# Two-stage attention and a gated short convolution on one core: output products as four 32-channel column strips, last stores joined, another order

## The chip, the cores and the metric

The kernel runs on one core of one Trainium2 chip. The metric is the device time of one execution in microseconds, lower is better. The program has one launch; host code only brings the inputs into another layout.

## The reference, cut to what matters

`B, N, C = 4, 12800, 128`, 32 inducing points, all in f32:

```python
def mab(q, kv):
    s = scale * (q @ kv.transpose(0, 2, 1)); s = s - s.max(-1, keepdims=True)
    a = np.exp(s); a /= a.sum(-1, keepdims=True) + 1e-09
    return a @ kv
h = mab(I, x)            # 32 inducing points attend to all tokens: (4, 32, 128)
y = mab(x, h)            # each token attends to the 32 rows of h: (4, 12800, 128)
gate_pre = sum(conv_w[k] * y_shifted_by(4 - k) for k in range(5))
out = (sigmoid(gate_pre) * (y @ w_val)) @ w_out
```

## The kernel before, in words

Each batch's 12800 tokens are four strips of 3200 (`R = 4`), which lie side by side on the partitions, 32 partitions to a strip. The 3200 are cut into 7 or 8 chunks (`SIZES`, 128 to 512 tokens of each strip); there are 29 chunks `k` over the four batches.

Per batch: `s1` makes the first scores of a chunk (f32, four matmuls of 32 columns, one to each token strip), DVE copies them out with their maximum; `gm` takes the maximum over a group of chunks (`GROUPS`) on POOL; `e1`/`h` take the exponential on ACT, transpose 32 x 32 blocks on DVE and multiply with x (again 32-column strips). `x` turns x on PE for batch 0, later batches load it in both layouts. `u`, `t`, `w`, `W` (`prep` to `prep3`) make h, its transpose hT, and the weights W that carry h, the convolution and the value projection; `po` (`prep_out`) scales the output weights and splits them into f16 high and low parts. `s2` makes the second scores of a chunk (f32 strips) and sends them down a chain: DVE transpose and maximum (L697, L702), POOL subtract (L708), ACT exponential (L714), DVE sum (L720), POOL multiply (L731), DVE transpose (L737), ACT and POOL split into f16 high and low parts P1 and P2 (L742, L749).

A row block `r` (`rblock`, two per chunk) multiplies W with shifted P in matmuls of 32 rows by 128 columns, four at a time on the four row groups: 15 terms of the gate (L763) and 3 of the value (L772). ACT takes the tanh (L833), DVE multiplies gate and value (`gv`, L843), ACT and POOL split that into f16 parts gh and gl (L856, L861).

`o` (`outp`) is the output product of one token strip of a chunk: three f16 terms, 128 rows by 128 columns (L881 to L883), for the last chunk one f32 product (L874). ACT or DVE (`OUTV` says which) copies it out of PSUM with its scale (L893, L891), and SP stores it (L898). So PE has three tile shapes, which the planner calls full (128 x 128), rows (32 x 128) and strips (128 x 32).

The order is a planner's. PE runs the items of the table `ORDER` as they stand; `z` is a run of dummy products on zeros (first number: its name, second: how many). All other engines get their order from a list schedule with assumed durations, due times and the biases `URGE`; `AHEAD` bounds how early loads go. Each engine runs its queue strictly in that order and waits on semaphores.

Of the kernel before, what the change touches and what calls it, by code (L numbers as in the profile page):

```python
# [20 lines left out]
P = 128  # L21
# [28 lines left out]
class Plan:  # L50
# [85 lines left out]
    def lay(self, deps, succ, topo, nominal):  # L136
# [18 lines left out]
        while len(seq) < n:  # L155
# [14 lines left out]
            if e == "SP":  # L170
                bus = max(bus, start) + ops[i]["dur"]
                end[i] = max(bus, start + 0.5) + (1.7 if start < 10.0 else 2.6)
                free[e] = start + 0.4
# [39 lines left out]
def tile_kernel(ctx: ExitStack, tc: tile.TileContext, xt, xk, indT_in, w64, out):  # L213
# [288 lines left out]
    def prep(b):  # L502
# [27 lines left out]
        i2 = PE(0.21 * len(gs) + 0.05, f3, [i0] + [ix["sum", b, c] for c in range(len(SIZES[b]))], [key], Hs + Ds, lag=0.2)  # L530
# [28 lines left out]
    def prep2(b):  # L559
# [4 lines left out]
        def f4():  # L564
            T.matmul(pt(key)[:, :M], c_["wval"], st["hT", b], start=True, stop=True)

        i4 = PE(0.28, f4, [ix["hT", b], iw], [key], [("hT", b)], lag=0.15)
# [46 lines left out]
    def prep3(b, e):  # L614
# [8 lines left out]
        i6 = PE(0.35, f6, ix[w2][e], [key], [w2], lag=0.25)  # L623
# [240 lines left out]

    def outp(k, r):
        b, c = seqs[k]
        n, p, q = SIZES[b][c], r // 2, r % 2
        g1, g2, tg = ("gh", b, c, p), ("gl", b, c, p), ("tg", b, c, p)
        key, os = ("a", "o", b, c, r), ("os", b, c, r)
        if k >= len(seqs) - 2:  # L870
            os = ("ss" if k == len(seqs) - 1 else ("et", "et", "et", "pt")[r], "out", b, c, r)
        if k == len(seqs) - 1:
            def f():
                T.matmul(pt(key)[:, :n], st["wof", b], st[tg][:, q, :n], start=True, stop=True)  # L874

            i = PE(1.06 / 512 * n, f, [ix["gv", b, c, r], ix["wo", b]], [key], [tg, ("wof", b)])
        else:
            def f():
                t = pt(key)[:, :n]
                w = st["wo", b]  # L880
                T.matmul(t, w[:, 0], st[g1][:, q, :n], start=True, stop=False)  # L881
                T.matmul(t, w[:, 1], st[g1][:, q, :n], start=False, stop=False)  # L882
                T.matmul(t, w[:, 0], st[g2][:, q, :n], start=False, stop=True)  # L883

            i = PE(COST["out"] * n, f, [ix[g2], ix["wo", b]], [key], [g1, g2, ("wo", b)])
        v = 4 * k + r in OUTV

        def ev():
            o, a = sb(pw, os, [P, 512])[:, :n], st[key][:, :n]
            if v:  # L890
                V.tensor_scalar(o, a, st["osc", b], None, ALU.mult)  # L891
            else:
                S.activation(o, a, AF.Copy, scale=st["osc", b])  # L893

        j = op("DVE" if v else "ACT", cost("psum", n) + 0.07 if v else cost("act", n) + 0.06, ev, [i], 0.0, [os], [key, ("osc", b)])

        def store():
            nc.sync.dma_start(out[b, :, r, FIRST[b][c]:FIRST[b][c] + n], st[os][:, :n])  # L898

        op("SP", n * 512 / BW, store, [j], 0.0, [], [os])  # L900


# [7 lines left out]
    def idle(k, n):  # L910
# [3 lines left out]
        def f():  # L914
            t = pt(key, (P, 2, 512))[:, 0]
            for _ in range(n):
                T.matmul(t, c_["zero"][:, :P], c_["zero"], start=True, stop=True)  # L917

        PE(0.216 * n, f, [], [key])
# [36 lines left out]
GROUPS = [[[0, 1], [2, 3, 4], [5, 6, 7]], [[0, 1, 2, 3], [4, 5, 6]], [[0, 1, 2], [3, 4, 5, 6]], [[0, 1, 2], [3, 4, 5, 6]]]  # L956
ORDER = [
# [40 lines left out]
]  # L998
XEV = ["SSSV", "SVSS", "SVSS", "SSSV", "SSSS", "SSVS", "SVSS", "SSVS"]
URGE = {  # L1000
    "e1.f": -13,
    "s2.sub": 8,
# [81 lines left out]
```

## Time and profile before

| | us |
|---|---|
| three runs | 287.75, 288.19, 290.25 |
| median | 288.19 |
| the profiled execution | 288.69 |
| its span (first to last instruction) | 286.6 |
| PE, DVE, POOL, ACT busy | 278.0, 230.4, 214.2, 204.6 |

In the lines of the profile, PE is TensorE's matmuls, PEld its weight loads, DVE VectorE, ACT ScalarE, POOL GpSimd, SP the engine that issues most DMAs. A row in order of time has start and length in us, engine, line, operation, what it writes and reads, tile rows*columns, shape and count; in brackets stands the idle time ahead of it and what ended it. A matmul's length is longer than its share of PE's time, since matmuls overlap: the distance between starts is what counts. A row in 20 us stretches has the busy time of PE, PEld, DVE, ACT and POOL, then the granted clock, the DMA share and GB/s.

### The profile page before, as it was taken

What the parts mean: (1) busy time and instruction counts of PE and PEld (TensorE: products, weight loads), DVE (VectorE), ACT (ScalarE), POOL (GpSimd) and SP (SyncE); (2) the same over time, 40 slices, a digit from 0 to 9 for tenths busy, and PEclk for the clock granted to TensorE, in tenths of its full rate; (3) what the DMA queues carried; (4) which work ended last, traced back from release to release, by engine and by line L of the source; (5) the groups of instructions that cost most, each with busy time, mean ns of one, the idle gap of its engine ahead of it and who ended that gap; (6) DMA issues with size and microseconds to landing.
All of it is one profiled execution on the core that took longest, in us unless ns stands there. A gap on an engine that the chain in (4) does not pass through costs nothing.

```text
span 286.6 us, 10022 instructions
## 1 busy us (share of the span) xinstructions
PE 278.0 (97%) x4038; PEld 136.0 (47%) x4038; DVE 230.4 (80%) x574; ACT 204.6 (71%) x310; POOL 214.2 (75%) x256
## 2 busy tenths in 40 slices
PE   8899999999999999999999999999999999999992
PEld 3467546464335335555454645644334443433450
DVE  1458899999999999769789899897896986844551
ACT  2363344578785769767787579897799787888792
POOL 1122077887899989959498989998899999865770
PEclk9999999999999999999999999999999999999998
DMA  7999999999987979998647993234233343443545
GB/s 250 408 418 421 415 387 365 414 392 395 361 314 234 403 274 294 413 363 267 239 160 234 342 387 109 106 125 159 88 132 130 129 148 128 156 146 148 189 159 194
DMA packets 24382, 74.50 MB, mean 260 GB/s; under 512 B 2832, under 2 KB 12560, under 8 KB 22160
## 3 DMA queue, kind: packets, MB, share of 16 engines
q1 hardware_dynamic: 24192, 73.84, 69.0%
q8 instruction: 32, 0.52, 0.7%
q14 instruction: 14, 0.11, 0.1%
q10 hardware_dynamic: 144, 0.02, 0.0%
HBM read 47.63 MB, written 26.21 MB: 258 GB/s over the span
## 4 chain that ended last, share of the span: by engine, by line
PE 90%; DVE 4%; DMA 3%; issue 0%; SPq 0%; ACT 0%
PE g L763 29%; PE a L881 10%; PE a L486 8%; PE a L691 8%; PE a L883 7%; PE a L882 7%; PE a L772 7%; PE a L422 7%; PE g L397 3%; DMA xt<-in_xt_dram 3%; PE g L917 2%; PE a L621 1%; DVE ss L430 1%; DVE e L697 1%; PE a L528 1%; PE a L874 0%
## 5 line engine op out<-in xcount | busy, mean ns | idle before, releaser
L861 POOL TENSOR_TENSOR gl<-tg,gh 128x1024 f16<-128x1024 f32 (+4 forms) x56 | 106.5, 1906 | 18.0 <-ACT gh L856 15.7
L763 PE MATMUL g<-P,W 32*128 32x448 f16 (+5 forms) x1740 | 109.7, 345 | 0.0
L833 ACT ACTIVATE tg<-g,gsc 128x1024 f32<-128x1024 f32 (+5 forms) x58 | 57.8, 996 | 29.4 <-PE g L763 24.9
L843 DVE SCALAR_TENSOR_TENSOR tg<-tg,a 128x512 f32<-128x512 f32 (+5 forms) x116 | 65.5, 602 | 11.7 <-PE a L772 10.8
L763 PEld LDWEIGHTS <-W 32*128 32x128 f16 x1740 | 50.6, 92 | 43.2 <-issue 13.1
L856 ACT CAST gh<-tg 128x1024 f16<-128x1024 f32 (+4 forms) x56 | 52.7, 946 | 0.6 <-PE a L882 0.2
L772 PE MATMUL a<-P,W 32*128 32x512 f16 (+5 forms) x348 | 42.7, 348 | 0.0
L893 ACT ACTIVATE os<-a,osc 128x512 f32<-128x512 f32 (+4 forms) x63 | 38.1, 633 | 5.5 <-PE a L883 5.3
L881 PE MATMUL a<-gh,wo 128*128 128x512 f16 (+4 forms) x112 | 40.2, 359 | 0.0
L882 PE MATMUL a<-gh,wo 128*128 128x512 f16 (+4 forms) x112 | 39.6, 354 | 0.0
L883 PE MATMUL a<-gl,wo 128*128 128x512 f16 (+4 forms) x112 | 39.6, 354 | 0.0
L891 DVE TENSOR_SCALAR os<-a,osc 128x448 f32<-128x448 f32 (+4 forms) x45 | 29.6, 674 | 7.8 <-PE a L883 7.4
L749 POOL TENSOR_TENSOR P<-pt,P 128x512 f16<-128x512 f32 (+4 forms) x29 | 29.9, 1038 | 2.6 <-ACT P L742 2.4
L731 POOL TENSOR_TENSOR e<-e,z 128x512 f32<-128x512 f32 (+4 forms) x29 | 27.1, 938 | 4.9 <-DVE z L723 2.5
L708 POOL TENSOR_TENSOR e<-e,m 128x512 f32<-128x512 f32 (+4 forms) x29 | 27.1, 938 | 3.1 <-DVE m L702 3.0
L422 PE MATMUL a<-xt,indT 128*32 128x512 f32 (+5 forms) x232 | 27.3, 540 | 1.3 <-DVE ss L430 0.9
L486 PE MATMUL a<-xk,et 128*32 128x129 f32 x800 | 28.1, 275 | 0.4 <-issue 0.3
L486 PEld LDWEIGHTS a<-xk,et 128*32 128x32 f32 x800 | 23.3, 109 | 8.2 <-issue 3.7
L691 PE MATMUL a<-xt,hT 128*32 128x512 f32 (+4 forms) x232 | 27.0, 544 | 0.0
L430 DVE TENSOR_SCALAR_CACHE_REDUCE ss<-a 128x512 f32<-128x512 f32 (+5 forms) x29 | 17.4, 603 | 11.9 <-PE a L422 11.6
L714 ACT ACTIVATE e<-e 128x512 f32<-128x512 f32 (+4 forms) x29 | 16.5, 576 | 10.5 <-POOL e L708 10.4
L881 PEld LDWEIGHTS <-wo 128*128 128x128 f16 x112 | 10.9, 97 | 27.4 <-issue 18.2
(107 smaller groups left out, 326.0 us busy)
## 6 DMA issues: line engine op xcount, KB each, us to landing
xt<-in_xt_dram SPq DMA_DIRECT2D x11, 1024.0 KB, 7.8
out_dram<-os SPq DMA_DIRECT2D x36, 256.0 KB, 3.8
xk<-in_xk_dram SPq DMA_DIRECT2D x10, 903.0 KB, 7.9
out_dram<-os SPq DMA_DIRECT2D x40, 224.0 KB, 2.4
xt<-in_xt_dram SPq DMA_DIRECT2D x8, 896.0 KB, 9.4
xk<-in_xk_dram SPq DMA_DIRECT2D x6, 1032.0 KB, 8.5
xt<-in_xt_dram SPq DMA_DIRECT2D x6, 960.0 KB, 8.0
xk<-in_xk_dram SPq DMA_DIRECT2D x5, 967.5 KB, 9.7
```

Source lines behind the costliest of these rows:

```text
L422: T.matmul(s[32 * r:32 * r + 32, :n], c_["indT"], x[:, o:o + n // 32, r, :], start=True, stop=True)
L486: T.matmul(t[32 * s:32 * s + 32, :P + 1], e[:, 32 * i:32 * i + 32], x[:, m + i, :], start=i < R, stop=i >= nb - R)
L691: T.matmul(s[32 * r:32 * r + 32, :n], st["hT", b], x[:, m:m + nb, r, :], start=True, stop=True)
L763: T.matmul(st[f"g{r // 2}", b, c][:, r % 2, :n], st["W", b][q, w, k, :], st[("P1", "P2")[e]][q, o:o + n], start=u == 0, stop=u == len(taps ...
L772: T.matmul(st["a", "v", b, c, r][:, :n], st["W", b][q, w, TAPS, :], st[("P1", "P2")[e]][q, o:o + n], start=u == 0, stop=u == 2)
L833: S.activation(t[:, :, :n], st[f"g{p}", b, c][:, :, :n], AF.Tanh, scale=st["gsc", b])
L843: V.scalar_tensor_tensor(t, t, 1.0, st["a", "v", b, c, r][:, :n], ALU.add, ALU.mult)
L856: S.copy(sb(pw, g1, [P, 2, 512], F16)[:, :, :n], st[tg][:, :, :n])
L861: G.tensor_tensor(sb(pw, g2, [P, 2, 512], F16)[:, :, :n], st[tg][:, :, :n], st[g1][:, :, :n], ALU.subtract)
L881: T.matmul(t, w[:, 0], st[g1][:, q, :n], start=True, stop=False)
L882: T.matmul(t, w[:, 1], st[g1][:, q, :n], start=False, stop=False)
L883: T.matmul(t, w[:, 0], st[g2][:, q, :n], start=False, stop=True)
```

## The change

An output product is cut by channels into four column strips of 32, so that it has the shape of the scores; so are the small products of `prep2` (`wval` by hT), and the dummy products have 32 columns. The output of the last chunk goes into one tile per pair of strips and out by two stores in place of four; of the last chunk but one, the stores of strips that ACT copies are issued by ACT. `ORDER` and its companions (`GROUPS`, `XEV`, `URGE`, `OUTV`, `AHEAD`) are another set, and the planner's tables say "strips" for the products that changed.

```diff
+    def columns(t, terms):
+        for j, (w, x) in enumerate(terms):
+            for r in range(R):
+                T.matmul(t[32 * r:32 * r + 32], w[:, 32 * r:32 * r + 32], x, start=j == 0, stop=j == len(terms) - 1)
...
-                T.matmul(t, w[:, 0], st[g1][:, q, :n], start=True, stop=False)
-                T.matmul(t, w[:, 1], st[g1][:, q, :n], start=False, stop=False)
-                T.matmul(t, w[:, 0], st[g2][:, q, :n], start=False, stop=True)
+                columns(t, [(w[:, 0], st[g1][:, q, :n]), (w[:, 1], st[g1][:, q, :n]), (w[:, 0], st[g2][:, q, :n])])
...
+        if last:
+            if q:
+                def store():
+                    nc.sync.dma_start(out[b, :, r - 1:r + 1, FIRST[b][c]:FIRST[b][c] + n],
+                                      st[os][:, :2 * n].rearrange("p (r t) -> p r t", r=2))
...
+        elif k == len(seqs) - 2 and not v:
+            def store():
+                S.dma_start(out[b, :, r, FIRST[b][c]:FIRST[b][c] + n], st[os][:, :n])
...
-                T.matmul(t, c_["zero"][:, :P], c_["zero"], start=True, stop=True)
+                T.matmul(t[:M], c_["zero"][:, :M], c_["zero"], start=True, stop=True)
...
-GROUPS = [[[0, 1], [2, 3, 4], [5, 6, 7]], [[0, 1, 2, 3], [4, 5, 6]], [[0, 1, 2], [3, 4, 5, 6]], [[0, 1, 2], [3, 4, 5, 6]]]
+GROUPS = [[[0, 1, 2], [3, 4], [5, 6, 7]], [[0, 1, 2, 3], [4, 5, 6]], [[0, 1, 2], [3, 4, 5, 6]], [[0, 1, 2], [3, 4, 5, 6]]]
...
-    ("W", 2, 0), ("o", 11, 0), ("r", 13, 0), ("h", 3, 0), ("h", 3, 1), ("s1", 3, 6), ("s2", 2, 6), ("s2", 2, 4),
+    ("s2", 2, 2), ("r", 12, 0), ("o", 10, 2), ("o", 10, 3), ("o", 11, 0), ("o", 11, 1), ("h", 3, 0), ("s1", 3, 5),
+    ("s2", 2, 5), ("h", 3, 1), ("s2", 2, 4), ("l", 1, 2), ("s1", 3, 4), ("r", 12, 1), ("s1", 3, 6), ("s2", 2, 6),
...
-AHEAD = 19
+AHEAD = 25
```

Three places show what the change does to the queues. The first is PE in the middle of the program. Before, the last term of an output of batch 1 is followed by the second scores of batch 2 and a row block:

```order
L882 MATMUL a<-gh,wo 128x448
L883 LDWEIGHTS wo
L883 MATMUL a<-gl,wo 128x448
L691 MATMUL a<-xt,hT 32x480 x4
L763 LDWEIGHTS W
L763 MATMUL g_3042<-P_94,W 128x448
```

After, at the row block r(12,1) (the first number of a shape is the columns of the tile):

```order
L869 MATMUL a<-gl,wo 32x448
L486 MATMUL a<-xk,et 32x129 x15
L422 MATMUL a<-xt,indT 32x512 x4
L691 MATMUL a<-xt,hT 32x480 x4
L486 MATMUL a<-xk,et 32x129 x16
L691 MATMUL a<-xt,hT 32x448 x4
L422 MATMUL a<-xt,indT 32x512 x4
L772 LDWEIGHTS W
L772 MATMUL a<-P_94,W 128x448
```

Before, full, strips and rows follow each other; after, output, h, s1 and s2 are one run of strips up to the rows, and h, s1 and s2 stand here that stood behind r(13,0).

The second is DVE in the head, between hT of batch 0 and the first row block. Before (`e_603` and `e_623` are the second scores of chunks 0 and 1 of batch 0, `ss` the first scores of batch 1):

```order
L723 RECIPROCAL z_670<-z_670 128x8
L702 TENSOR_REDUCE m2_674<-e_667 128x16
L737 STREAM_TRANSPOSE pt_702<-e_603 128x160
L470 STREAM_TRANSPOSE et_710<-ss_529 128x448
L629 COPY W_713<-a_677 128x768
L697 STREAM_TRANSPOSE e_721<-a_704 128x512
L737 STREAM_TRANSPOSE pt_724<-e_623 128x256
```

After (`e_589` is chunk 1, `e_609` chunk 0):

```order
L702 TENSOR_REDUCE m2_715<-e_706 128x16
L470 STREAM_TRANSPOSE et_724<-ss_467 128x448
L470 STREAM_TRANSPOSE et_728<-ss_546 128x448
L470 STREAM_TRANSPOSE et_736<-ss_510 128x448
L737 STREAM_TRANSPOSE pt_739<-e_589 128x256
L737 STREAM_TRANSPOSE pt_756<-e_609 128x160
```

Three transposes of batch 1 moved ahead of the two that end the chain of chunks 1 and 0, and chunk 1 goes ahead of chunk 0.

The third is the tail, SP's last stores before:

```order
L898 DMA out_0_dram<-et_5761 128x512
L898 DMA out_0_dram<-ss_5767 128x160
L898 DMA out_0_dram<-ss_5772 128x160
L898 DMA out_0_dram<-ss_5774 128x160
L898 DMA out_0_dram<-ss_5781 128x160
L898 DMA out_0_dram<-et_5789 128x512
L898 DMA out_0_dram<-pt_5796 128x512
L898 DMA out_0_dram<-et_5799 128x512
```

and after, SP's:

```order
L924 DMA out_0_dram<-et_6762 128x512
L912 DMA out_0_dram<-ss_6777 128x2x160
L924 DMA out_0_dram<-et_6808 128x512
L912 DMA out_0_dram<-ss_6745 128x2x160
```

with two stores that went from SP to ACT's queue, where one copy stands ahead of the last of them:

```order
L905 ACTIVATE ss_6777<-a_6772,osc_4707 128x160
L918 DMA out_0_dram<-et_6769 128x512
L905 ACTIVATE pt_6815<-a_6794,osc_4707 128x512
L905 ACTIVATE ss_6745<-a_6810,osc_4707 128x160
L918 DMA out_0_dram<-pt_6815 128x512
```

More of the change, by code (lines that the diff above doesn't have):

```diff
@@ L172, in lay @@
                 end[i] = max(bus, start + 0.5) + (1.7 if start < 10.0 else 2.6)
-                free[e] = start + 0.4
+                free[e] = start + 0.45
             seq.append(i)
@@ L528, in f3 @@
                 T.matmul(t[:M, :P + 1], st[Ds[g]], st[Hs[g]], start=g == 0, stop=g == gs[-1])
-        i2 = PE(0.21 * len(gs) + 0.05, f3, [i0] + [ix["sum", b, c] for c in range(len(SIZES[b]))], [key], Hs + Ds, lag=0.2)
+        i2 = PE(0.21 * len(gs) + 0.05, f3, [i0] + [ix["sum", b, c] for c in range(len(SIZES[b]))], [key], Hs + Ds, "strips", lag=0.2)
         def f4():
@@ L564, in f4 @@
         def f4():
-            T.matmul(pt(key)[:, :M], c_["wval"], st["hT", b], start=True, stop=True)
-        i4 = PE(0.28, f4, [ix["hT", b], iw], [key], [("hT", b)], lag=0.15)
+            columns(pt(key)[:, :M], [(c_["wval"], st["hT", b])])
+        i4 = PE(0.28, f4, [ix["hT", b], iw], [key], [("hT", b)], "strips", lag=0.15)
         def g0():
@@ L621, in f6 @@
                     T.transpose(t[32 * r:32 * r + 32, q, :], st[w2][:, e, q, :], c_["ident"])
-        i6 = PE(0.35, f6, ix[w2][e], [key], [w2], lag=0.25)
+        i6 = PE(0.35, f6, ix[w2][e], [key], [w2], "strips", lag=0.25)
         def f7():
@@ L869, in outp @@
         key, os = ("a", "o", b, c, r), ("os", b, c, r)
-        if k >= len(seqs) - 2:
-            os = ("ss" if k == len(seqs) - 1 else ("et", "et", "et", "pt")[r], "out", b, c, r)
-        if k == len(seqs) - 1:
+        last = k == len(seqs) - 1
+        if last:
+            os = ("ss", "out", b, c, p)
+        elif k == len(seqs) - 2:
+            os = (("et", "et", "et", "pt")[r], "out", b, c, r)
+        if last:
             def f():
-                T.matmul(pt(key)[:, :n], st["wof", b], st[tg][:, q, :n], start=True, stop=True)
-            i = PE(1.06 / 512 * n, f, [ix["gv", b, c, r], ix["wo", b]], [key], [tg, ("wof", b)])
+                columns(pt(key)[:, :n], [(st["wof", b], st[tg][:, q, :n])])
+            i = PE(1.06 / 512 * n, f, [ix["gv", b, c, r], ix["wo", b]], [key], [tg, ("wof", b)], "strips")
         else:
@@ L880, in f @@
                 w = st["wo", b]
[L881 to L885, printed above, removed]
+                columns(t, [(w[:, 0], st[g1][:, q, :n]), (w[:, 1], st[g1][:, q, :n]), (w[:, 0], st[g2][:, q, :n])])
+            i = PE(COST["out"] * n, f, [ix[g2], ix["wo", b]], [key], [g1, g2, ("wo", b)], "strips")
         v = 4 * k + r in OUTV
+        new = not last or q == 0
         def ev():
-            o, a = sb(pw, os, [P, 512])[:, :n], st[key][:, :n]
+            if new:
+                sb(pw, os, [P, 512])
+            at = q * n if last else 0
+            o, a = st[os][:, at:at + n], st[key][:, :n]
             if v:
@@ L893, in ev, with store @@
                 S.activation(o, a, AF.Copy, scale=st["osc", b])
[L895 to L900, printed above, removed]
+        j = ix["out", k, r] = op("DVE" if v else "ACT", cost("psum", n) + 0.07 if v else cost("act", n) + 0.06, ev, [i], 0.0,
+                                 [os] * new, [key, ("osc", b)] + [os] * (not new))
+        if last:
+            if q:
+                def store():
+                    nc.sync.dma_start(out[b, :, r - 1:r + 1, FIRST[b][c]:FIRST[b][c] + n],
+                                      st[os][:, :2 * n].rearrange("p (r t) -> p r t", r=2))
+                op("SP", 2 * n * 512 / BW, store, [ix["out", k, r - 1], j], 0.0, [], [os])
+        elif k == len(seqs) - 2 and not v:
+            def store():
+                S.dma_start(out[b, :, r, FIRST[b][c]:FIRST[b][c] + n], st[os][:, :n])
+            j = op("ACT", 0.45, store, [j], 0.0, [], [os], lag=2.3)
+            op("NOP", 0.0, lambda: None, [j])
+        else:
+            def store():
+                nc.sync.dma_start(out[b, :, r, FIRST[b][c]:FIRST[b][c] + n], st[os][:, :n])
+            op("SP", n * 512 / BW, store, [j], 0.0, [], [os])
     def warm_up():
@@ L916, in f @@
             for _ in range(n):
-                T.matmul(t, c_["zero"][:, :P], c_["zero"], start=True, stop=True)
-        PE(0.216 * n, f, [], [key])
+                T.matmul(t[:M], c_["zero"][:, :M], c_["zero"], start=True, stop=True)
+        PE(0.216 * n, f, [], [key], kind="strips")
     def S1(b, c, bank="a"):
@@ L953, in tile_kernel @@
     return plan
-GROUPS = [[[0, 1], [2, 3, 4], [5, 6, 7]], [[0, 1, 2, 3], [4, 5, 6]], [[0, 1, 2], [3, 4, 5, 6]], [[0, 1, 2], [3, 4, 5, 6]]]
+GROUPS = [[[0, 1, 2], [3, 4], [5, 6, 7]], [[0, 1, 2, 3], [4, 5, 6]], [[0, 1, 2], [3, 4, 5, 6]], [[0, 1, 2], [3, 4, 5, 6]]]
 ORDER = [
[40 rows of a table removed]
[40 rows of a table added]
 ]
-XEV = ["SSSV", "SVSS", "SVSS", "SSSV", "SSSS", "SSVS", "SVSS", "SSVS"]
+XEV = ["SVVV", "SSSV", "SVSV", "SSSS", "SSSS", "SSVS", "SSSS", "SSSS"]
 URGE = {
-    "e1.f": -13,
-    "s2.sub": 8,
-    "s2.hi": -28,
-    "s2.lo": 7.5,
-    "s2.tout": -6.5,
-    "s2.ex": 1.5,
-    "s2.tin": -3.5,
-    "rblock.gv": -5,
-    "s2.sm": -2.5,
-    "make_xk.ev": 1.5,
-    "h.acc": -4,
-    "halves.lo": -1,
-    "s2.mx": 5.5,
-    "s1.g": -5.5,
-    "s2.nm": -3,
-    "halves.hi": -2,
-    "e1.tr": -4.5,
-    "evac.ev": -20.5,
-    "rblock.th": 8,
-    "values.gv": -4,
-    "rows.th": -8,
-    "gmax.f1": 4,
-    "gmax.f0": 1,
-    "outp.ev": 4,
+    "e1.f": -3,
+    "s2.sub": 14,
+    "s2.hi": -37.5,
+    "s2.lo": -0.5,
+    "s2.tout": -6,
+    "s2.ex": 3,
+    "s2.tin": 0.5,
+    "rblock.gv": -5,
+    "s2.sm": -2,
+    "make_xk.ev": 14,
+    "h.acc": -2,
+    "halves.lo": -0.5,
+    "s2.mx": 4.5,
+    "s1.g": -6.5,
+    "s2.nm": 9.5,
+    "halves.hi": -3,
+    "e1.tr": -2.5,
+    "evac.ev": -18.5,
+    "rblock.th": 9,
+    "values.gv": 5,
+    "rows.th": -6.5,
+    "gmax.f1": 28,
+    "gmax.f0": 1.5,
+    "outp.ev": 18,
 }
 TURNED = (0,)
-EVEN = 0.04765998428116873
+EVEN = 0.0469045735303122
 OUTV = [
[4 rows of a table removed]
[5 rows of a table added]
 ]
```

86 rows, old and new, of tables (ORDER, OUTV) are left out of this document.

## The prediction

> **What bounds the kernel now.** I read the page first (busy time, slices, the chain that ended last), then the stretches of 20 us, then the order of time on each engine.
>
> ```profile
> span 286.6 us, 10022 instructions
> PE 278.0 (97%) x4038; PEld 136.0 (47%) x4038; DVE 230.4 (80%) x574; ACT 204.6 (71%) x310; POOL 214.2 (75%) x256
> PEclk9999999999999999999999999999999999999998
> PE 90%; DVE 4%; DMA 3%; issue 0%; SPq 0%; ACT 0%
> ```
>
> The matrix engine is busy for 97% of the span, at the full granted clock, and the chain that ended last lies on it for 90%. So an edit is worth what it takes off PE, as long as no other engine comes to set PE's pace. Which one could is in the stretches (columns: PE, PEld, DVE, ACT, POOL):
>
> ```profile
> 40.00:60.00 20.00, 19.56 (x418) 11.20 (x415) 19.07 (x56) 10.64 (x22) 15.33 (x29) 1.00 0.98 390
> 60.00:80.00 20.00, 20.00 (x299) 9.49 (x302) 19.13 (x51) 15.39 (x27) 16.50 (x20) 1.00 1.01 377
> 80.00:100.00 20.00, 20.00 (x274) 8.42 (x270) 19.36 (x47) 14.32 (x20) 19.04 (x17) 1.00 0.86 312
> 120.00:140.00 20.00, 20.00 (x347) 10.39 (x335) 15.94 (x44) 14.40 (x23) 14.13 (x18) 1.00 0.92 323
> ```
>
> PE has no idle time from 60 us on, but in 40 to 100 us DVE is idle for only 2.4 us of 60: there it is nearly a second bound. In 120 to 140 us it has 4.1 us to spare.
>
> **Term 1: the changes of tile shape.** PE works in three shapes: full (outputs, transposes of x), rows (gate and value products, L763 and L772) and strips (scores, h, the turned weights). Between two shapes it stops:
>
> ```profile
> 149.91 0.35 PE L883 MATMUL a<-gl,wo 128*128 128x448 f16 x1
> 150.19 1.01 PE L691 MATMUL a<-xt,hT 128*32 128x480 f32 x8
> 151.72 1.30 PE L763 MATMUL g<-P,W 32*128 32x448 f16 x24
> 152.96 0.36 PE L881 MATMUL a<-gh,wo 128*128 128x448 f16 x1
> 154.29 0.35 PE L882 MATMUL a<-gh,wo 128*128 128x448 f16 x1
> 154.48 0.35 PE L883 MATMUL a<-gl,wo 128*128 128x448 f16 x1
> 154.76 0.36 PE L772 MATMUL a<-P,W 32*128 32x448 f16 x2
> 156.65 0.52 PE L621 MATMUL a<-ident,w 128*32 128x128 f16 x24
> 157.10 0.36 PE L881 MATMUL a<-gh,wo 128*128 128x448 f16 x1
> ```
>
> Within a shape a 448-wide product follows its predecessor after 0.19 us (154.29 to 154.48). From full to strips it takes 0.28 (149.91 to 150.19), so the change costs 0.09; from full to rows 0.28 (154.48 to 154.76), again 0.09; from rows to full, the 24 row products are six rounds of four, 6 x 0.19 = 1.14, and 1.24 pass to the output product: 0.10. From strips to full 0.45 pass, of which six rounds of 0.058 (worked out below) are work: 0.10.
>
> Now the price of an output product in strips: three terms by four strips, 12 matmuls in place of 3. It is unchanged only if four strips run at once, with their weight loads hidden. The trace has that form with the same data type, 128 rows by 32 columns in f16, in the turned weights:
>
> ```profile
> 41.90 0.52 PE L621 MATMUL a<-ident,w 128*32 128x128 f16 x24
> 42.25 1.89 PE L691 MATMUL a<-xt,hT 128*32 128x512 f32 x16
> 43.97 0.51 PE L621 MATMUL a<-ident,w 128*32 128x128 f16 x24
> L621 PEld LDWEIGHTS <-w 128*32 128x32 f16 x192 | 3.3, 96 | 3.1 <-issue 2.4 <-POOL e L708 0.3
> 56.60 0.22 PE L882 MATMUL a<-gh,wo 128*128 128x128 f16 x1
> 56.66 0.22 PE L883 MATMUL a<-gl,wo 128*128 128x128 f16 x1
> ```
>
> 24 strips of 128 columns take 0.35 us (41.90 to 42.25), six rounds of 0.058; one full product of 128 columns takes 0.06 (56.60 to 56.66). So four strips cost one full product, though each had its own weight load of 96 ns. The f32 strips that follow start with no gap: the data type alone costs nothing, which is what lets outputs join s1, s2 and h. I take the 336 rounds of the outputs at their old price. Bounds: 0, and for loads that don't hide, 336 x 0.096 = 32 us (a rival below).
>
> [...]
>
> Read from end to end in the two programs' orders, PE changes shape 169 times before (28 full to strips, 25 strips to full, 18 strips to rows, 15 rows to strips, 40 full to rows, 43 rows to full) and 131 times after (7, 6, 59, 59, 0, 0). I take 0.10 for each, as the two that remain (rows and strips) have it: 38 fewer are 3.8 us, 0.7 of it ahead of the first row block (19 changes against 12) and **3.1 us behind it**, where PE hardly waits, so these count in full. Bounds: at 0.09 out of full, 0.10 out of rows and 0.11 out of strips (the rows have two decimals) it is 16.7 against 13.7, 3.0 in all; at 0.11 throughout 4.2.
>
> **Term 2: the head.** The new order has 21 dummy products (`z`) for 31. Each is 0.22 us (18 of them fill 37.91 to 41.90 below), so 2.2 us of PE work go. Whether the time goes is decided by the first row block r(-1,1), which needs the probabilities P of chunk 0 and both halves of W:
>
> ```profile
> 35.47 0.28 POOL L456 TENSOR_SCALAR m<-m 64x1 f32<-64x1 f32 x1 [7.50 <-DVE m L441]
> 35.63 0.19 DVE L548 COPY hT<-a 128x32 f32<-128x32 f32 x1 [0.34 <-PE a L545]
> 36.20 1.00 POOL L450 TENSOR_SCALAR ng<-m 32x1 f32<-32x1 f32 x4
> 37.23 1.23 ACT L465 ACTIVATE ss<-ss,ng 128x448 f32<-128x448 f32 x2 [5.77 <-POOL ng L450]
> 37.91 4.06 PE L917 MATMUL g<-zero 128*128 128x512 f16 x18
> 42.21 0.60 DVE L470 STREAM_TRANSPOSE et<-ss 128x448 f32<-128x448 f32 x1
> 43.21 0.49 POOL L749 TENSOR_TENSOR P<-pt,P 128x160 f16<-128x160 f32 x1
> 44.00 0.40 DVE L737 STREAM_TRANSPOSE pt<-e 128x256 f32<-128x256 f32 x1
> 44.43 0.41 ACT L742 CAST P<-pt 128x256 f16<-128x256 f32 x1 [0.52 <-DVE pt L737]
> 44.92 0.67 POOL L749 TENSOR_TENSOR P<-pt,P 128x256 f16<-128x256 f32 x1 [1.22 <-ACT P L742]
> 46.14 1.02 PE L763 MATMUL g<-P,W 32*128 32x128 f16 x42
> ```
>
> Before, hT is there at 35.82 and P of chunk 0 at 43.70, 7.9 us later; r(-1,1) starts at 46.14. After, u comes earlier: four dummies (0.9) and one s1 chunk (0.75 by the 0.43 of a 512-wide f32 round, two rounds, scaled) less stand ahead of it, and the weights' load now lies ahead of the last x load; I take 1.4 us, hT at 34.4. But chunk 0's chain is longer: s2(0,1) goes first; POOL has the maximum of batch 1 (gm, 0.73 + 1.00) in the middle; ACT has four exponentials (0.62 each) ahead of P's casts; and DVE has three transposes L470 in a row ahead of L737. Counted from hT: the maximum enters POOL at about 4.1, ends at 5.8, the third exponential at 7.6; the three L470 fill 7.0 to 8.8; two L737 (0.4 and somewhat less) to 9.5; the casts to 9.9; the two L749 (0.67, 0.49) to **10.8**. So r(-1,1) starts at about 45.3: **0.85 us** gained of the 3.0 that the head could give (2.2 + 0.7 + 0.1 of other work moved). PE waits there for about 2 us, with only the rest of its queue behind it. Bounds: -3.0 (the chain is no longer than before) and +0.8 (it is 1.6 longer than counted). I take 0.85, since the queue orders are known and the durations are rows.
>
> **Term 3: the tail.**
>
> ```profile
> 280.93 0.38 PE L883 MATMUL a<-gl,wo 128*128 128x512 f16 x1
> 281.35 0.69 ACT L893 ACTIVATE et<-a,osc 128x512 f32<-128x512 f32 x1 [0.61 <-PE a L883]
> 279.23 2.81 SPq L898 DMA_DIRECT2D out_dram<-ss  x4
> 283.08 0.41 SPq L898 DMA_DIRECT2D out_dram<-et  x1
> out_dram<-et SPq DMA_DIRECT2D x3, 256.0 KB, 2.4
> out_dram<-ss SPq DMA_DIRECT2D x4, 80.0 KB, 3.2
> ```
>
> Before, PE's last product streams out at 281.15 (280.93 + 0.22). ACT's copy ends 0.9 later, but the last store is issued only at 283.08, behind a queue on SP that four small stores (2.81 us) had made; it lands after about 2.4, 4.4 us behind PE. After, two joined stores replace four, and two stores go out from ACT. The last work is o(28,1): its copy waits on ACT behind a 512-wide one (0.69), and ends about 1.0 behind PE; SP is free and issues at once. The joined store is of the small kind (3.2): 4.2 behind PE. **0.3 us** gained; between -1.0 (landing like the big ones, 2.4) and +0.5 (twice the rows of a small one, somewhat slower landing). An ACT-issued store holds ACT for about the 0.4 of these issues, with one copy queued behind it.
>
> **Term 4: other engines.** Their work is the same in sum (three more copies on DVE, one transposed block fewer). In 40 to 100 us DVE is the cover: PE gets some 1.3 us faster there by 13 or so fewer changes, and DVE has 2.4 us of idle time. I charge nothing; if the cover fails it is rival C.
>
> **The sum**: 3.1 + 0.85 + 0.3 = 4.25 off the profiled execution, whose own time is 288.69 (span 286.6 and 2.1 around it): 284.4. The median of the runs shown is 288.19, 0.5 below it, so in that frame **283.9**.
>
> **The rivals** (times in the median's frame).
> - B, the head keeps its whole gain: P of chunk 0 comes after 8 us as before. Another 2.2 us: 281.7. For it: before, z(2,18) ran on past the point at which the turned weights were ready. Against: the three L470 that now stand ahead.
> - C, DVE sets the pace between 46 and 100 us: the 1.3 us of that stretch and the head's 0.85 are lost: 286.1. For it: 19.1 to 19.4 of 20 busy. Against: DVE's queue has no more work ahead of each row block there than before.
> - D, the other side: ahead of r(12,1) stand now two s1, two s2 and two h that stood behind r(13,0). By their DVE work (transposes and reductions of about 0.6 to 0.7, nine or ten of them) gv of chunk 12 moves back by some 6 us. If DVE's idle time ahead (4.1 in 120 to 140) can't take any of it, since its inputs come too late, outputs of chunk 12 stall and PE with them: 283.9 + 6 = 290. It decides once less than 2 us of the 6 find idle time. Against: two row blocks lie between gv and those outputs.
> - E, the strips' loads stand open: 283.9 + 32 = 316. That is also the case in which the change doesn't do what it says. The rounds of L621 speak against it; they are 128 wide, and only more time is there at 512.
>
> **How the numbers follow.** My forecast 0.54 (own range 283.0 to 285.6), B 0.14, C 0.21, D 0.08, E 0.03. About 1%, 2.9 us, is what a measurement here can tell from no change: faster than 285.3 are most of the forecast and B (0.64), slower than 291.1 are a part of D, and E (0.06); the rest is within (0.30). The range from 281.5 to 287.6 takes in the forecast, most of B, and C, with the bounds of the tail.
>
> **What would show it.** Output products as 32-column strips whose rounds of four start 0.19 (448) or 0.22 us (512) apart; no gap where they meet s1, s2, h; gaps of about 0.1 only at row blocks, 59 each way; r(-1,1) near 45.3 us, with PE idle ahead of it; last store landing some 4.2 us behind PE. Rounds longer than 0.22 us mean E; idle PE ahead of row blocks in 46 to 100 us means C, around chunk 12 D. An idle PE in the last 80 us would be a thing that I have not foreseen.

## The result, and the profile after

The changed kernel takes 286.82 us in the median of 20 runs (284.49 to 288.74), the kernel before 288.97 beside it: ratio **0.9914, 95% interval 0.989 to 0.9938**, 2.5 us faster. The prediction had 4.3 us. The profiled execution took 286.78. From its page (the total, busy times, the chain, two groups, the queue of instruction packets, of which before had `32, 0.52, 0.7%`):

```profile
span 285.0 us, 12107 instructions
PE 274.5 (96%) x5084; PEld 141.1 (49%) x5084; DVE 231.3 (81%) x577; ACT 203.5 (71%) x307; POOL 214.5 (75%) x256
q8 instruction: 40, 0.66, 0.9%
PE 87%; DVE 6%; ACT 3%; issue 2%; POOL 1%; DVEq 0%; ACTq 0%; POOLq 0%
L869 PE MATMUL a<-gh,wo 128*32 128x448 f16 (+4 forms) x896 | 63.2, 356 | 0.0
L869 PEld LDWEIGHTS <-wo 128*32 128x32 f16 x1344 | 33.4, 96 | 36.0 <-issue 17.1
```

PE's busy time fell by 3.5 us (278.0 to 274.5), the span by 1.6 only: PE is now idle at times. The stretches of 20 us show where (PE, PEld, DVE, ACT, POOL, clock, DMA share, GB/s); before, PE was busy for all 20.00 in each but the first:

```profile
40.00:60.00 20.00, 19.63 (x379) 10.89 (x376) 18.52 (x55) 10.68 (x24) 15.51 (x32) 1.00 0.96 385
60.00:80.00 20.00, 19.66 (x386) 10.47 (x386) 18.82 (x51) 15.38 (x26) 17.02 (x20) 1.00 0.92 336
80.00:100.00 20.00, 19.70 (x373) 8.77 (x362) 19.56 (x49) 15.15 (x21) 17.00 (x17) 1.00 0.94 337
120.00:140.00 20.00, 20.00 (x438) 11.68 (x432) 18.55 (x49) 13.70 (x22) 17.23 (x20) 1.00 0.78 284
140.00:160.00 20.00, 19.70 (x386) 9.95 (x382) 17.78 (x48) 13.93 (x22) 16.73 (x23) 1.00 0.98 347
```

The strips themselves came as forecast. In order of time on PE:

```profile
152.06 0.36 PE L869 MATMUL a<-gl,wo 128*32 128x448 f16 x4
152.25 0.55 PE L869 MATMUL a<-gh,wo 128*32 128x448 f16 x8
152.62 0.36 PE L869 MATMUL a<-gl,wo 128*32 128x448 f16 x4
153.76 0.36 PE L869 MATMUL a<-gl,wo 128*32 128x448 f16 x4
153.95 0.94 PE L486 MATMUL a<-xk,et 128*32 128x129 f32 x27
```

Four strips of 448 take 0.19 us (152.06 to 152.25), as one full product did, and `h` follows them with no gap (153.76 to 153.95). The trace has 131 shape changes, as counted. What is new are waits of PE:

```profile
52.28 0.62 PE L691 MATMUL a<-xt,hT 128*32 128x512 f32 x1 [0.31 <-issue]
69.20 0.96 PE L422 MATMUL a<-xt,indT 128*32 128x448 f32 x8 [0.34 <-DVE z L723]
100.24 0.61 PE L763 MATMUL g<-P,W 32*128 32x512 f16 x7 [0.55 <-issue]
158.59 1.06 PE L422 MATMUL a<-xt,indT 128*32 128x512 f32 x8 [0.30 <-DVE e L697]
213.58 1.39 PE L763 MATMUL g<-P,W 32*128 32x480 f16 x24 [0.45 <-ACT tg L833]
```

The brackets count from the modelled end of the matmul ahead. Counted from the start that its width and shape would give (0.19 us for 448 columns, 0.10 for a change) these five are 0.48, 0.51, 0.70, 0.47 and 0.61 us.

The profile puts the waits at 69.20 and 158.59 down to DVE, because a semaphore of DVE's changed last (69.14, 158.51). But PE's sequencer stood at a semaphore of the loads of x until the last part of a load landed, at 69.07 and 158.46. The same products wait in two kernels described below, the changed one with the old stores and the one with a shorter maximum, and there the profile names the load:

```profile
69.51 0.96 PE L422 MATMUL a<-xt,indT 128*32 128x448 f32 x8 [0.84 <-DMA xt<-in_xt_dram]
157.50 1.07 PE L422 MATMUL a<-xt,indT 128*32 128x512 f32 x8 [0.35 <-DMA xt<-in_xt_dram]
```

Ahead of r(-1,1), PE is not idle. Products of `h` fill the time up to it, and POOL's last split of P ends at 45.36:

```profile
34.89 0.19 DVE L548 COPY hT<-a 128x32 f32<-128x32 f32 x1 [0.40 <-PE a L545]
42.89 2.33 PE L486 MATMUL a<-xk,et 128*32 128x129 f32 x56
44.24 1.12 POOL L749 TENSOR_TENSOR P<-pt,P 128x256 f16<-128x256 f32 x2 [1.22 <-ACT P L742]
45.15 0.71 PE L763 MATMUL g<-P,W 32*128 32x128 f16 x12
```

All waits of more than 0.09 us behind r(-1,1), summed by the count from starts, are 1.3 us before and 3.9 after. The table gives such sums for one profiled execution each ("lost" is that sum, "tail" the span's end less the end of PE's last product). Single executions differ: with a shorter maximum on DVE (below), the third column is 234.1 for the changed kernel and 236.1 for the new order alone, where these rows have 235.1 for both. So a few tenths between two rows show nothing.

| kernel | r(-1,1) starts | from there to PE's end | lost | tail | span |
|---|---|---|---|---|---|
| before | 46.14 | 235.2 | 1.3 | 5.2 | 286.6 |
| after | 45.15 | 235.1 | 3.9 | 4.7 | 285.0 |
| strips alone, old order | 45.34 | 232.3 | 2.0 | 6.2 | 283.9 |
| new order alone, full products | 44.72 | 235.1 | 1.4 | 4.1 | 283.9 |
| mixed, new order | 44.64 | 233.5 | 2.6 | 4.0 | 282.2 |
| mixed, old order | 45.23 | 232.2 | 1.8 | 4.3 | 281.7 |

### The profile page after: what moved, and what is told of

It is laid out like the page before. It is cut to its first block, busy times and chain, and to the rows that moved or that the text cites. A ratio compares the mean times of both kernels' runs of the same rounds, so it can differ in the third digit from the quotient of the medians.

```text
span 285.0 us, 12107 instructions
## 1 busy us (share of the span) xinstructions
PE 274.5 (96%) x5084; PEld 141.1 (49%) x5084; DVE 231.3 (81%) x577; ACT 203.5 (71%) x307; POOL 214.5 (75%) x256
## 4 chain that ended last, share of the span: by engine, by line
PE 87%; DVE 6%; ACT 3%; issue 2%; POOL 1%; DVEq 0%; ACTq 0%; POOLq 0%
PE g L763 29%; PE a L869 24%; PE a L772 7%; PE a L486 7%; PE a L691 7%; PE a L422 7%; PE g L397 2%; PE g L943 2%; PE a L932 1%; DVE ss L430 1%; PE a L621 1%; DVE tg L843 1%; ACT xk L402 1%; DVE os L903 1%; DVE z L720 1%
## 5 line engine op out<-in xcount | busy, mean ns | idle before, releaser
L763 PEld LDWEIGHTS <-W 32*128 32x128 f16 x1740 | 51.0, 92 | 44.7 <-issue 15.1
L869 PE MATMUL a<-gh,wo 128*32 128x448 f16 (+4 forms) x896 | 63.2, 356 | 0.0
L869 PEld LDWEIGHTS <-wo 128*32 128x32 f16 x1344 | 33.4, 96 | 36.0 <-issue 17.1
L869 PE MATMUL a<-gl,wo 128*32 128x512 f16 (+4 forms) x448 | 42.5, 354 | 0.0
L905 ACT ACTIVATE os<-a,osc 128x448 f32<-128x448 f32 (+4 forms) x60 | 36.7, 633 | 6.8 <-PE a L869 6.2
L903 DVE TENSOR_SCALAR os<-a,osc 128x448 f32<-128x448 f32 (+4 forms) x48 | 31.6, 674 | 11.4 <-PE a L869 10.1
L691 PE MATMUL a<-xt,hT 128*32 128x512 f32 (+4 forms) x232 | 28.0, 541 | 0.3 <-issue 0.3
L772 PEld LDWEIGHTS <-W 32*128 32x128 f16 x348 | 12.3, 92 | 17.6 <-issue 12.8
```

The costliest lines, as they stand in the source:

```text
L691: T.matmul(s[32 * r:32 * r + 32, :n], st["hT", b], x[:, m:m + nb, r, :], start=True, stop=True)
L763: T.matmul(st[f"g{r // 2}", b, c][:, r % 2, :n], st["W", b][q, w, k, :], st[("P1", "P2")[e]][q, o:o + n], start=u == 0, stop=u == len(taps ...
L772: T.matmul(st["a", "v", b, c, r][:, :n], st["W", b][q, w, TAPS, :], st[("P1", "P2")[e]][q, o:o + n], start=u == 0, stop=u == 2)
L869: T.matmul(t[32 * r:32 * r + 32], w[:, 32 * r:32 * r + 32], x, start=j == 0, stop=j == len(terms) - 1)
```

## The experiments

**The change taken apart.** Four kernels on one chip, the kernel before at 288.52.

Strips alone: the kernel before, same order on every engine, with `columns` in it.

```diff
-                T.matmul(t, w[:, 0], st[g1][:, q, :n], start=True, stop=False)
...
+                columns(t, [(w[:, 0], st[g1][:, q, :n]), (w[:, 1], st[g1][:, q, :n]), (w[:, 0], st[g2][:, q, :n])])
```

> The kernel of before with every full product that the change cuts (outputs, wval by hT, dummies) in 32-column strips; the order table, the planner's numbers and so all queues of DVE, ACT, POOL and SP stay as before. PE changes shape 132 times for 169. Theory 1 (the strips save 0.1 us at each change that goes, and it is the new order that adds waits): 3 to 3.7 us less, ratio 0.987 to 0.990, PE waits hardly more than before. Theory 2 (DVE and POOL pace PE in whatever order, so what PE saves comes back as waits): at most 1.5 us less, ratio 0.995 or above, with new waits of PE between 40 and 240 us.

New order alone: the changed kernel with that line undone.

> The changed kernel with full products in place of strips; its order table, stores and all other queues stay. PE changes shape about 165 times for 131. Theory 1: about 3.4 us slower than the changed kernel, so 1.002 to 1.004 of before: the new order alone is worth nothing or less. Theory 2: the changes that come back disappear in waits that are there anyway, within 1.5 us of the changed kernel, 0.992 to 0.997 of before.

The stores alone, taken out of the changed kernel, and put into the one before:

```diff
-                nc.sync.dma_start(out[b, :, r, FIRST[b][c]:FIRST[b][c] + n], st[os][:, :n])
+                    nc.sync.dma_start(out[b, :, r - 1:r + 1, FIRST[b][c]:FIRST[b][c] + n], ...)
+                S.dma_start(out[b, :, r, FIRST[b][c]:FIRST[b][c] + n], st[os][:, :n])
```

> The changed kernel with the last stores as before: four small stores and all of them from SP. If the joined stores are worth the 0.3 us of the prediction: 0.3 us slower than the changed kernel, about 0.9925 of before, and the last landing some 4.4 us behind PE's last product. If they are worth nothing or cost something: 0.990 to 0.9915.

> The kernel of before with the joined stores and the ACT-issued ones alone; PE's order is that of before, which ends on a 512-wide output. Prediction: 0.3 us less, ratio 0.999; with the last store issued from ACT as soon as its copy ends, up to 1.0 us less, 0.9965. Nothing: 1.000.

| kernel | median, us | ratio to before, 95% |
|---|---|---|
| strips alone | 286.45 | 0.9926 [0.9901, 0.9952] |
| new order alone | 286.13 | 0.9917 [0.9895, 0.994] |
| changed kernel, old stores | 285.96 | 0.9901 [0.9879, 0.9924] |
| old kernel, new stores | 288.55 | 1.0001 [0.998, 1.0021] |

Each half gives what both give together (0.9914), and the stores nothing that can be measured. Neither theory foretold this: the first had the new order alone at 1.002 or more, the second the strips alone at 0.995 or more. But in the profile the strips alone took 2.8 us off PE behind r(-1,1), and 1.0 of it was lost in the tail (6.2 us for 5.2). The stores on SP's queue, in the kernel with strips alone:

```profile
275.64 3.71 SPq L902 DMA_DIRECT2D out_dram<-ss  x4
279.45 0.38 SPq L902 DMA_DIRECT2D out_dram<-et  x1
280.40 0.41 SPq L902 DMA_DIRECT2D out_dram<-et  x1
```

An issue usually takes 0.33 to 0.42 us (145 of 168 before, 139 of 164 after); four took 3.71. One of them started at 276.12 and ended at 278.41, and between 276.23 and 278.04 lies a packet of queue 8, that of instructions. Strips bring 1050 matmuls and as many weight loads more; the packets rise from 32 to 40, where PE's instructions rise from 8139 to 10230: one packet to 254 and 256 of them. Here is a third theory ("fetch"; "pace" is the second, that the other engines set PE's pace): the extra instructions cost time, where PE's program comes late and where its fetching holds up SP. That is a guess: the profile shows the packets, PE's idle time and the long issues, but no view says what PE or SP waited for there.

**More instructions without strips.** Half of the row products issued as two of half the columns: as many instructions as the strips add, the same shapes.

```diff
+        for i, j in ((0, n // 2), (n // 2, n)) if u % 2 or u == 2 else ((0, n),):
-        T.matmul(st[f"g{r // 2}", b, c][:, r % 2, :n], st["W", b][q, w, k, :], st[("P1", "P2")[e]][q, o:o + n],
+            T.matmul(st[f"g{r // 2}", b, c][:, r % 2, i:j], st["W", b][q, w, k, :], st[("P1", "P2")[e]][q, o + i:o + j],
```

> The kernel before, in which half of the row blocks' products (those of one of the 32-row tiles with odd tap index, and a few others) are issued as two products of half the columns: about 2090 more instructions of PE, as many as the strips bring, with the same products, the same tile shapes, the same order on every engine and no shape change less. Theory pace (the strips' saving is lost because other engines cannot follow): ratio 0.999 to 1.002, no new stall of PE. Theory fetch (the strips' extra instructions cost time through the fetching of PE's program): 1.002 to 1.006, that is 0.6 to 1.7 us slower, with stalls of PE that no semaphore ends, of 0.3 us and more, in 50 to 105 us, and 40 fetch packets instead of 32.

> The same halving of products in the new order with full output products: the instructions of the changed kernel without its strips. Theory pace: 0.991 to 0.993, as the new order with full products alone (0.9917). Theory fetch: 0.994 to 0.998, slower than that kernel by 0.6 to 1.7 us.

Measured: 294.99 us, 1.0231 [1.0195, 1.0266] in the old order, four times the expected loss, and 289.83, 1.0035 [1.0008, 1.0063] in the new. PE in the new order with halved products, in order of time:

```profile
51.67 0.74 PE L764 MATMUL g<-P,W 32*128 32x128 f16 x30 [1.06 <-issue]
58.02 0.23 PE L774 MATMUL a<-P,W 32*128 32x128 f16 x2 [0.53 <-issue]
```

and in the old order:

```profile
53.50 0.52 PE L764 MATMUL g<-P,W 32*128 32x128 f16 x11 [3.24 <-issue]
```

PE waits, for no semaphore, in the middle of a row block. In the old order its time behind r(-1,1) rose by 7.1 us (242.3), 4.1 of them in such waits; where the other 3.0 went was not taken apart. The new order with full and unhalved products has no such wait. The control halves products only behind 105 us:

```diff
-        for i, j in ((0, n // 2), (n // 2, n)) if u % 2 or u == 2 else ((0, n),):
+        for i, j in ((0, n // 2), (n // 2, n)) if seqs.index((b, c)) > 6 and (u % 2 or u == 2) else ((0, n),):
```

> The new order with whole output products and halved row products, as in the run that halved them everywhere (1.0035), but only for the chunks behind the seventh, so behind about 105 us: 1580 of the 2090 extra instructions stay. Theory fetch: the stalls at 51 and 58 us (1.9 us in that run) are gone, and what the halving itself costs stays for three quarters: 0.993 to 0.998. If halving had cost that run its time by itself and not by late instructions, three quarters of the difference to the new order with whole products (0.9917) would stay: 0.999 to 1.002.

Measured 288.03 us, 0.9967 [0.9945, 0.999]: within the third theory's range, though its interval reaches the edge of the other's. No stall stands in it at 51 or 58 us; 0.9 us of PE's time behind r(-1,1) remain in its profile as the halving's own cost (236.0 for 235.1).

**Is it DVE after all?** DVE's maximum (L702) over 4 of 32 scores.

```diff
-            V.tensor_reduce(sb(pw, mk, [P, 16, 1])[:, :nb, 0], st[ek][:, :nb], AX.X, ALU.max)
+            V.tensor_reduce(sb(pw, mk, [P, 16, 1])[:, :nb, 0], st[ek][:, :nb, :4], AX.X, ALU.max)
```

> The changed kernel, with DVE's maximum of the scores taken over the first 4 of 32 instead of over all (each of 29 reductions of 0.63 us falls to about 0.15, some 14 us of DVE's work gone; a different but near maximum is subtracted). Theory pace: PE's waits behind its first row block fall from 4.7 to about 2 us, ratio to the kernel before 0.984 to 0.988. Theory fetch: 0.990 to 0.993, as the changed kernel itself (0.9914).

> The same shorter maximum in the new order with full output products. Theory pace: this kernel has no saving that could come back as a wait, so little is gained: 0.989 to 0.992, and the changed kernel with the shorter maximum is ahead of it by 1 us or more. Theory fetch: 0.990 to 0.993, and the two with the shorter maximum are level within 0.6 us.

DVE lost 9.1 us of work, not 14:

```profile
PE 273.4 (96%) x5084; PEld 140.8 (50%) x5084; DVE 222.2 (78%) x577; ACT 203.3 (71%) x307; POOL 214.5 (75%) x256
```

The times stayed: 285.93, 0.9901 [0.9868, 0.9934] with strips, 286.25, 0.992 [0.9893, 0.9946] without, 0.3 us apart, where that theory had 1 us or more. So it is not DVE's pace that takes most of the strips' gain.

**Strips only where they pay.** A list `WHOLE` keeps outputs whole in the new order; every other engine's queue is that of the changed kernel.

```diff
+            if whole:
+                T.matmul(t, w, x, start=j == 0, stop=j == len(terms) - 1)
+                continue
...
+                columns(t, [...], 4 * k + r in WHOLE)
```

> The changed kernel with strips only for the outputs of the first seven chunks (k up to 6, all before about 105 us) and whole output products behind: of the 35 shape changes that strips save in the new order 16 are saved, with 500 of the 2000 extra instructions. Theory fetch (the extra instructions cost stalls of PE where its program arrives late, at 50 to 60 and near 100 us): the 1.6 us saved are given back there, 0.990 to 0.994, level with the new order with whole products (0.9917). Theory of full count: 0.984 to 0.988.

> The opposite: whole products for the first seven chunks, strips for all later ones: 19 of 35 shape changes saved, with 1500 of the 2000 extra instructions, all behind about 105 us. Theory fetch: the stretch of 50 to 105 us is free of new stalls, and the 1.9 us count in full: 0.983 to 0.987. Theory pace (what PE saves returns as waits for the other engines): 0.990 to 0.993.

> The changed kernel with strips only for the 55 outputs of 116 that stand between two row blocks together with scores, transposes or the like; the 61 outputs whose neighbours are outputs alone are whole again, so all 35 shape changes stay saved with half of the extra instructions (some 35 or 36 fetch packets instead of 40). Theory fetch: faster than the changed kernel by 0.5 to 1.5 us, 0.986 to 0.990. Theory pace: as the changed kernel, 0.990 to 0.993.

> Both restrictions: strips only for the 38 outputs behind the seventh chunk that stand beside other column products; 19 shape changes saved with 700 extra instructions. Theory fetch: 0.983 to 0.987, the best of the four with the late one. Theory pace: 0.990 to 0.993.

| strips for | packets | median, us | ratio to before, 95% |
|---|---|---|---|
| first seven chunks | 34 | 286.83 | 0.9924 [0.9898, 0.995] |
| later chunks | 38 | 286.01 | 0.9889 [0.9857, 0.992] |
| mixed: outputs beside other column products | 35 | 283.99 | **0.982** [0.9788, 0.9852] |
| those of them in later chunks | 34 | 284.61 | 0.9843 [0.9807, 0.9878] |

The early strips gain nothing over the new order alone (0.9917), though they save 12 changes behind r(-1,1). The later ones gain less than expected: PE needs 1.1 us less behind r(-1,1) (234.0 for 235.1), but the tail is 0.9 longer (5.0 us). The mixed kernel keeps all 131 changes with half of the extra instructions; it is faster than expected, and its interval lies clear of the changed kernel's. Lines of its page, and PE's order of time at the places of the two stalls:

```profile
span 282.2 us, 11033 instructions
PE 273.4 (97%) x4547; PEld 140.6 (50%) x4547; DVE 231.3 (82%) x577; ACT 203.4 (72%) x307; POOL 214.4 (76%) x256
q8 instruction: 35, 0.57, 0.9%
51.68 0.59 PE L691 MATMUL a<-xt,hT 128*32 128x512 f32 x1
51.75 2.08 PE L422 MATMUL a<-xt,indT 128*32 128x480 f32 x13
97.20 1.68 PE L763 MATMUL g<-P,W 32*128 32x512 f16 x28
98.81 0.62 PE L872 MATMUL a<-gh,wo 128*32 128x512 f16 x8
```

Where the changed kernel's 40 products before 100.78 were broken off for 0.70 us, 28 of them run through here (97.20 to 98.81). Set against each other product by product, the mixed kernel draws ahead by 0.7 us between 52 and 59 and 0.9 near 100, where PE has none of those stalls (busy for 20.00 us of 80 to 100, the changed kernel for 19.70), and 0.5 at 158, where its load of x had landed in time (155.65). It had 0.5 from the head, and loses 0.5 near 115. At 68 both wait for a load of x. Of the 2.8 us between the two spans, 1.6 lie behind r(-1,1), and 0.7 in the tail, where the changed kernel has a packet (278.53 to 279.46) and one of SP's issues, from 279.19 on, took 0.65 us.

Last, the same rule in the old order:

```diff
+                columns(t, [(w[:, 0], st[g1][:, q, :n]), ...], 4 * k + r in WHOLE)
```

> The order of before, untouched on every engine, with strips only for the 58 outputs that stand between two row blocks beside other column products, whole products for the others: all shape changes stay saved that strips save in this order, with half of the extra instructions. Theory fetch: faster than strips everywhere in this order (0.9926) by 0.5 to 1.5 us: 0.986 to 0.991. If what the mixed kernel gained in the new order came of something else in that order (its waits), nothing changes here: 0.991 to 0.995.

Measured 284.03 us, 0.9844 [0.982, 0.9868], better than expected, and 2.4 us under strips everywhere in that order. PE had no part in that: 232.2 us for 232.3, its last product ended at 277.42 for 277.67. The tail had. SP's queue:

```profile
275.33 1.84 SPq L905 DMA_DIRECT2D out_dram<-ss  x4
277.27 0.38 SPq L905 DMA_DIRECT2D out_dram<-et  x1
278.21 0.41 SPq L905 DMA_DIRECT2D out_dram<-et  x1
```

No packet falls among the last stores here; the last is issued 2.2 us earlier (278.21 for 280.40). In the kernel before one does (280.74 to 281.67): one issue took 1.34 us, which is in the prediction's row of 2.81 for the four. So of these three profiles in the old order the two with a packet among the last stores have the longer tails, 6.2 us (strips everywhere) and 5.2 (before) for 4.3. The kernel before has the fewest instructions, and a packet there all the same.

## Why the prediction was right or wrong

- **Term 1, the price: right.** There are 131 changes, and the rounds cost what they did. In the old order the saving came out whole: 3.0 us from r(-1,1) to PE's end (mixed, 235.2 to 232.2) for 34 changes fewer, 0.09 each; the forecast was 3.1 for 31. Rival E did not come: 1344 weight loads of 96 ns stand under rounds of 0.19.
- **Term 1, "where PE hardly waits, so these count in full": the step that failed.** Waits on "issue" and waits for the loads of x stood in no term. From r(-1,1) to PE's end the changed kernel took 235.1 us for 235.2: the whole 3.1 came back. The waits are 2.6 of it by the count from starts (3.9 less 1.3): 0.9 on "issue" (0.48 at 52.28, 0.15 at 59.04 and 0.70 at 100.24, less 0.43 at 53.55 before), 1.0 for the two loads of x (69.20, 158.59), 0.6 for a tanh (213.58). The tanh's wait stands in the new order alone too (0.60), so it belongs to the order. The new order alone also took 235.1, with full products. Set against it product by product, the changed kernel gains some 3.6 us where shape changes are gone, and loses as much: 1.35 between 50.5 and 54.3, 0.9 at 100.24, 0.65 and 0.5 at the loads of x, 0.2 at 45.4. The stall at 52.28 is 0.55 of the 1.35. The other 0.8 goes at the score products without an idle row, and it goes there as well with full products and the shorter maximum, so that the strips bring it is not shown. The loads of x are not shown to be the strips' doing either: the kernel with mixed strips in later chunks alone has full products up to 105 us, and waits 0.83 for another load of x at 66.56. So the stalls on "issue" are 1.45 of the 3.6 (0.55 and 0.9); neither the new order alone nor the mixed kernel has them at these places. Why the rest came back in this execution stays open. I had counted matmuls for PE's time, and never instructions.
- **Term 2, the head: the number came, 45.15 for 45.3, the account only in part.** hT came at 35.08 for 34.4, and the chain from it to the last split took 10.3 us for 10.8: two errors that nearly cancel. PE did not wait 2 us there; products of `h` filled the time. Kernels with that head started r(-1,1) between 44.6 and 45.5, so the closeness is luck; that they start 0.6 to 1.5 earlier than before is not. But strips in the old order start it at 45.34 and 45.23 as well, so not all of that is the new order's.
- **Term 3, the tail:** 0.5 in the profile for 0.3. Without a packet in the tail, the old stores take 4.3 us and the new ones 4.0 (the two mixed kernels), just the 0.3; but the old kernel's tail was 1.0 longer, with the issue of 1.34 us over a packet, which I took for the queue of small stores. In the old kernel with new stores an issue took 2.44 us, and they gained nothing.
- **Rivals:** C has nearly the time (286.1), but not its cause, as the shorter maximum shows. D did not come: the only wait near r(12,1) is the one at 158.59, just ahead of it, for a load of x and not for gv. Nor did B: the gain of the head is 1.0. Idle PE in the last 80 us, which I had called unforeseen, came at 213.58.
- **The sum:** 1.0 head, 0.1 behind it, 0.5 tail are the 1.6 of the profile's span; the medians give 2.2, the ratio 2.5.

## What to carry to other kernels

A form that cost the array nothing here (0.19 us a round, as the full product) brought 2091 instructions: price those too, and use the finer tiling only where it joins two pieces of work. Half the strips did all the good here, and 0.8 to 0.9% lay between strips everywhere and strips at the seams alone. Part of that may be luck of position: in the old order the tail was 6.2 us with an instruction packet among the last stores and 4.3 without. Where PE idles on "issue", look at which instruction of the program it stands: in two orders here it stood behind 724 matmuls. Where the profile names an engine for a wait, look whether a load landed at the same moment (69.07 us here, for DVE's 69.14).

## What the runs showed of the hardware

**PE stood idle on "issue" at certain places in its program.** Behind r(-1,1) that came once before, at 53.55 us (0.27 us by the brackets), and twice after, at 52.28 and 100.24 (0.31 and 0.55). These three ended 1.52, 1.25 and 1.28 us after the end of a packet of 16384 bytes on queue 8 (52.02, 51.03, 98.96). At 53.55 and at 52.28 PE had 724 matmuls behind it, though the orders differ, and at 100.24 it had 1613. Between the two lie 889 matmuls, with their loads 1778 instructions, seven times 254; there is one packet to 254 of PE's instructions before (32 for 8139) and one to 256 after (40 for 10230). That PE waits there for its program is inferred from this; no view shows it. Seven more such waits stand in the order of time of five other kernels: strips alone (57.94 and 69.52 us), halved products in the new order (51.67 and 58.02) and in the old (53.50, the longest with 3.24 us), mixed in the old order (58.08), and the shorter maximum with strips (99.13). In the changed kernel the DMA share is 0.92 to 0.96 from 40 to 100 us; but from 140 to 160 us it is 0.98 with no such stall. Why they fall between 51 and 101 us and not elsewhere stays open; that the loads of x have a part in it was not tried.

**Some of SP's DMA issues that overlap a packet of queue 8 took longer.** In the profiles of before and after 51 of SP's 332 issues overlap such a packet. 34 of them took the usual 0.33 to 0.42 us, but 11 took over 0.9 (0.93 to 1.49), and 9 of these ended 0.34 to 0.39 us after the packet's end. Of the 281 that met no packet, 3 took over 0.9. With strips alone one of the last stores' issues took 2.29 us (276.12 to 278.41), and ended 0.37 after the packet's end. What decides whether an issue is held stays open. Among the last stores it went with time: 1.9 us of tail between two kernels whose PE ended 0.25 us apart.
